# An opening in another order: when k is turned, how filter block 0 is transformed, and where square roots and means stand in GpSimd's queue

## The chip, the cores and the metric

The kernel runs on one core of a Trainium2 chip. The core has five engines with a queue each: TensorE (PE, matrix products; its weight loads are listed apart as PEld), VectorE (DVE), ScalarE (ACT), GpSimd (POOL) and SyncE (SP, which here only issues transfers). They wait for one another by semaphores, and each works through its own queue in order. The metric is the device time of one execution in microseconds; a comparison uses the median of several runs. The working dtype is bf16, sums are float32.

## The reference

Four layers follow one another on x of 2048 tokens by 576 channels: A, B, A, B, each added to its input after a layer norm.

```python
def _A_ref(q, k, v, shift_k, ssm_k, ssm_D):      # k, v, ssm_k, ssm_D are the same in both A layers
    k_shift = sum over 4 taps of k moved by t tokens * shift_k[:, tap]
    kv = k_shift * v
    y = causal convolution of kv with ssm_k along the 2048 tokens, by FFTs of length 4096
    return q * (y + kv * ssm_D)
def _B_ref(x, w_gate, w_up, w_down):             # 576 -> 4608 -> 576
    return (gelu(x @ w_gate) * (x @ w_up)) @ w_down
x = x + _A_ref(_layernorm(x), ...);  x = x + _B_ref(_layernorm(x), ...)    # and both once more
```

## The kernel before, in words

**Units.** The tokens are cut into four chunks of 512. A unit is one B layer of one chunk, eight in all: (layer 0, chunk 0), (0,1), (1,0), (1,1), (0,2), (0,3), (1,2), (1,3). They go in five passes (the first unit alone, three passes of two, the last alone); a pass has three phases, in which its units follow one another; in a phase 12 column groups of `w_gate` and `w_up` are multiplied (L1294, tile `gu`: 18 products each, two at a time in the two halves of the rows), ACT makes the gelu (L1298), DVE multiplies (L1299, tile `hT`), and `w_down` follows (L1311, tile `dn`), four token groups of 24 products, added to the residual `x_c` by DVE (L1345, in the last phase L1340). The first phase of the first unit is cut into two halves of the tokens (`first_half`, `half_gu`, L1228), so that it can begin with two of the four token groups, j = 0 and 2.

**The convolution.** Class `Conv` makes y, which depends on k, v and the filter alone, once per chunk, for both A layers. Chunk m is transformed by products with a twiddle table W (`fwd_full` L207: 8 products of 288 columns give one part, s = 0 or 1, of one of four frequency groups kt, and ACT evicts it, L209; `fwd_eo` L217 makes even and odd sums instead, 4 products for half the channels, from which DVE makes groups kt and kt + 2 by `cross`, L225). Transformed blocks of kv (`kc`) and of the filter (`h0`, `H1`, later `hc`) are multiplied on DVE (`prod`, L234 to L238) and inverted (`inverse`, L276). Blocks needed later are stored in HBM by POOL (L286) and come back as `kr` (L402) and `hr` (L410).

**The order** is written when the program is built. For the opening it is the text of `begin` and `first_half`. From the fourth pair of column groups on (after the change, the third) a planner (`fill`) keeps a rough clock for PE, DVE and ACT and takes from queues what it takes to be ready: `run_loads` (transfers; before the change as many as are ready at once), `run_v` (DVE work of the convolution), `run_p` (its PE work, with tiles from `cps`), `run_aq` and `run_vq` (norms and gates). PSUM is split into a pool `psp` of three tiles that `gu`, `dn` and most of the opening take in turn, and a pool `cps` of one.

**The opening before** (`begin`, L605 on; times of the profiled execution). PE: 32 products of 16 columns (L641), which only keep it busy; the taps' broadcasts (L645); 20 idle products with the identity (L655); the turn of k, 20 transposes (L670); the first half of filter block 0 turned (L690, tile `hps`, copied to `hT` by ACT, L691); the four taps of the short convolution (L565) in three groups; the second half of block 0 turned; then groups 0 and 2 of filter block 0 by even and odd sums (`h0_pair`, L739, with eight crosses on DVE), groups 0 and 2 of kv, and groups 1 and 3 of block 0 and of kv in full (L207); filter block 1 turned (L690); its group 2; the four inverses of chunk 0 (L276, mt = 0, 2, 1, 3).

**The tail of the opening.** For token group j: DVE's `gate` is two operations (L1163: x minus mean, times y; L1165: times rstd plus x, with the row sum). POOL's `mean` makes `nm` from the sum (L934). ACT's `sq` sums squares (L942). POOL's `root` is two operations (L949 `ve`, L950 `rstd`). DVE's `norm` makes `xn` (L1119, L1121), PE turns it (L1132, tile `xps`, after idle transposes L1129), and it is copied to `xnT` (L1140). Before the change `gate` issues its mean itself, and the queues stand thus:

```python
            head.gate(0, Y[0])
            head.gate(2, Y[2])
            head.sq(0)
            ...
            head.gate(1, Y[1])
            ...
            head.root(0)
            head.norm(0)
```

so that POOL has the means of groups 0, 2 and 1 ahead of the root of group 0. Last in `begin`, `head.more(3)` issues the load of the next chunk's x (`load_x(1)`, L889) on POOL, ahead of the roots of groups 1 and 3.

Of the kernel before, what the change touches and what calls it, by code (L numbers as in the profile page):

```python
# [16 lines left out]
ALU = mybir.AluOpType  # L17
# [66 lines left out]
class Conv:  # L84
# [9 lines left out]
    def __init__(self, tc, ctx, pace, A_k, A_v, A_shift_k, A_ssm_k, A_ssm_D, ident, psp, cpsp, ypool):  # L94
# [29 lines left out]
        self.startup = True  # L124
# [231 lines left out]
    def step(self, m, kv=None, loaded=False):  # L356
# [166 lines left out]
    def run_loads(self):  # L523
# [4 lines left out]
        while self.L and self.L[0][0]() <= t.pe - 0.3:  # L528
            self.L.popleft()[1]()
# [19 lines left out]
    def run_p(self):  # L549
# [4 lines left out]
        if max(ready(), self.ps_free) > t.pe:  # L554
            return False
        self.Pq.popleft()
        run()
        t.pe += cost
# [9 lines left out]
    def h1_rest(self):  # L568
# [26 lines left out]
        for s in range(2):  # L595
            for h in range(2):
                self.Pq.append((lambda: NEVER if self.neo >= N_EO else 0.0, 0.49, fwd(s, h)))
        for s in range(2):
            self.Pq.append((lambda: 0.0, 0.98, full(s)))

    def begin(self, head, tables):
# [4 lines left out]
        with ExitStack() as es:  # L606
# [4 lines left out]
            ones = tmp.tile([1, P], BF16, name="ones")  # L611
            warm = tmp.tile([P, 1], F32, name="warm")
# [13 lines left out]
            nc.scalar.dma_start(out=dvec[:], in_=self.sD.unsqueeze(0))  # L626
            nc.vector.memset(ones[:], 1.0)
# [11 lines left out]
            ps = self.ps()  # L639
            for _ in range(32):  # L640
                nc.tensor.matmul(ps[:, 0, 0:16], lhsT=ones[:], rhs=ones[:, 0:16], start=True, stop=True)  # L641
            for j in (3, 2, 1, 0):
# [3 lines left out]
                nc.scalar.copy(out=self.halves(self.skc[:, j, :]), in_=ps[:, :, 0:HW])  # L646
# [6 lines left out]
            ps = self.ps()  # L653
            for _ in range(20):
                nc.tensor.matmul(ps[:, 0, 0:P], lhsT=self.ident[:], rhs=self.ident[:], start=True, stop=True)  # L655
# [75 lines left out]
            def h0_pair(s, h):  # L731

                if s == 0 and h == 0:
                    h0[0] = self.hrp.tile([P, 2, D], BF16, tag="hr", name="h0")
                    h0[2] = self.krp.tile([P, 2, D], BF16, tag="kr", name="h0")
                ps = self.ps()
                for e in range(2):
                    for i in (e, e + 2):
                        nc.tensor.matmul(ps[:, e, 0:HW], lhsT=self.fwd_w(0, s, i), rhs=hT0[:, i, h * HW:(h + 1) * HW],  # L739
                                         start=(i == e), stop=(i == e + 2))  # L740
                eo = self.eop.tile([P, 2, HW], F32, tag="eo", name="eo")
                nc.scalar.copy(out=eo[:], in_=ps[:, :, 0:HW])
                cols = slice(h * HW, (h + 1) * HW)
                self.cross(eo, h0[0][:, s, cols], h0[2][:, s, cols])
                if s == 1 and h == 1:
                    for kt in (0, 2):
                        self.spill(self.Hd[0][kt], h0[kt])

# [9 lines left out]
            for s in range(2):  # L758
                for h in range(2):
                    h0_pair(s, h)  # L760
            kfwd(0)
            head.act_sum(2)
            head.act_sum(3)
            self.load_k(1, nc.gpsimd)
            head.stats(0)
            kfwd(2)
            kacc(0)
            head.act_sq(2)
            for s in range(2):
                h_part(0, 1, s)  # L770
            kfwd(1)
            head.stats(1)
            kacc(2)
            pair0(0, 0)
            head.act_sq(3)
            for s in range(2):
                h_part(0, 3, s)
            kfwd(3)
            self.load_v(1, nc.gpsimd)
            kacc(1)  # L780
            pair0(0, 1)
            self.hT1 = head.scratch([P, RT, D], "hT1")
# [7 lines left out]
            big = lambda: self.psp.tile([P, 2, 512], F32, tag="pr", name="ps")  # L790
            Y = {mt: inv0(mt, big()) for mt in (0, 2)}
            pair0(1, 1)
            Y[1] = inv0(1, big())
            Y[3] = inv0(3, self.cpsp.tile([P, 2, 512], F32, tag="cps", name="cps"))
# [605 lines left out]
```

## Time and profile before

| what | value |
|---|---|
| median of 3 runs | 946.57 us (945.75 to 946.74) |
| the profiled execution's own time | 949.34 us |
| its span, first to last instruction | 947.6 us |
| instructions in the profile | 19593 |
| first product of `w_gate` and `w_up` (L1228) | 46.19 us |
| first product of the second phase (L1294) | 93.67 us |
| DVE busy, ACT busy, POOL busy | 567.1, 292.8, 141.4 us |

The time of one execution is 1.74 us more than its span, for what lies around the first and the last instruction. A page of the profile names an instruction by the line of the kernel, its engine and its tiles (`out<-in`). The view of waits gives engine, line, what it waited for, and then the time in all, how often, and the longest wait. The chain is followed backwards from the last instruction: each piece is what ended last. The view by stretches gives for each stretch its length, the busy time of each engine with the number of instructions, and after them PEclk, the clock that TensorE was granted as a share of full speed.

### The profile page before, as it was taken

The page shows a single profiled execution, that of the slowest core. Times are in us where ns is not written, and L with a number is a line of the kernel's source. Part 1 is how long each engine was busy: PE and PEld are TensorE (multiplying, and loading weights), DVE is VectorE, ACT ScalarE, POOL GpSimd, SP SyncE. Part 2 cuts the span into 40 slices and gives each one's busy share as a digit, 9 for nine tenths or more (in the row PEclk, how much of TensorE's full clock was granted, in tenths as well). Part 3 has the DMA queues.
Part 4 walks back from the last instruction along what each step waited for, and adds up shares of the span by engine and source line. Part 5 has one row for each costly group of instructions (what it writes and reads, how often), then busy time and mean ns, then how long its engine had stood idle before and what let it go on. Part 6 is the DMA issues. An engine that isn't in the chain of part 4 may idle for free.

```text
span 947.6 us, 19593 instructions
## 1 busy us (share of the span) xinstructions
PE 930.1 (98%) x8380; PEld 547.3 (58%) x8380; DVE 567.1 (60%) x1032; ACT 292.8 (31%) x540; POOL 141.4 (15%) x305
## 2 busy tenths in 40 slices
PE   9899999999999998999999999999999999999998
PEld 6677455554654745656556556456456456556455
DVE  4879887888897346888888423763333334533332
ACT  5664315523124333331222521441211213311211
POOL 1433003602103005122010100130000002100000
PEclk9999999999999999999999999999999999999999
DMA  9939987977834515864960720692540540696630
GB/s 258 346 122 240 220 200 145 239 174 193 207 120 88 116 51 149 159 174 106 200 201 13 143 84 26 109 172 47 110 116 1 117 110 14 121 215 148 150 70 26
DMA packets 128491, 130.27 MB, mean 137 GB/s; under 512 B 43538, under 2 KB 120339, under 8 KB 128404
## 3 DMA queue, kind: packets, MB, share of 16 engines
q1 hardware_dynamic: 119232, 93.47, 46.5%
q0 software_dynamic: 9168, 35.54, 11.8%
q8 instruction: 65, 1.06, 0.5%
q14 instruction: 22, 0.18, 0.1%
q10 hardware_dynamic: 4, 0.01, 0.0%
HBM read 107.76 MB, written 11.80 MB: 126 GB/s over the span
## 4 chain that ended last, share of the span: by engine, by line
PE 92%; POOL 2%; DVE 2%; DMA 2%; issue 1%; ACT 1%; DVEq 0%
PE gu L1294 55%; PE dn L1311 27%; PE cps L217 2%; PE gu L1228 2%; DMA wd<-in_B_w_down_dram 2%; PE cps L276 1%; POOL rstd L950 1%; PE ps L207 1%; DVE x_c L1340 1%; PE cps L207 1%; POOL ve L949 0%; ACT junk L942 0%; DVE x_c L1165 0%; ACT hT L691 0%; DVE x_c L977 0%
## 5 line engine op out<-in xcount | busy, mean ns | idle before, releaser
L1294 PE MATMUL gu<-xnT,wgu 64*128 64x512 bf16 x4968 | 542.7, 377 | 4.4 <-DVE x_c L1340 4.4
L1294 PEld LDWEIGHTS <-wgu 64*128 64x128 bf16 x4968 | 244.1, 94 | 296.2 <-issue 12.9
L1298 ACT ACTIVATE ga<-gu 128x512 f32<-128x512 f32 x276 | 164.6, 597 | 522.8 <-PE gu L1294 512.1
L1299 DVE TENSOR_TENSOR hT<-ga,gu 128x512 bf16<-128x512 f32 x276 | 189.4, 686 | 213.4 <-ACT ga L1298 212.4
L1311 PE MATMUL dn<-wd,hT 128*128 128x288 bf16 x2304 | 295.3, 287 | 2.6 <-DMA wd<-in_B_w_down_dram 2.0
L1311 PEld LDWEIGHTS <-hT 128*128 128x128 bf16 x2304 | 224.0, 98 | 69.1 <-issue 12.7
L1345 DVE TENSOR_TENSOR x_c<-x_c,dn 128x576 f32<-128x576 f32 x64 | 48.2, 753 | 79.2 <-PE dn L1311 78.7
L934 POOL TENSOR_SCALAR nm<-s 128x1 f32<-128x1 f32 x62 | 20.3, 328 | 305.4 <-DVE x_c L1340 174.5
L942 ACT ACTIVATE junk<-x_c,nm 128x576 bf16<-128x576 f32 x48 | 37.0, 771 | 47.1 <-POOL nm L934 46.7
L950 POOL TENSOR_TENSOR rstd<-ve,neghalf_t 128x1 f32<-128x1 f32 x62 | 39.5, 637 | 5.2
L220 ACT ACTIVATE eo<-cps 128x576 f32<-128x576 f32 x44 | 28.5, 649 | 34.5 <-PE cps L217 30.1
L410 POOL DMA_DIRECT2D hr<-Hd x32 | 17.3, 539 | 138.6 <-DVE prod L237 138.6
L238 DVE TENSOR_TENSOR sum<-prod 128x576 bf16<-128x576 bf16 x72 | 33.0, 458 | 2.5
L1331 DVE TENSOR_TENSOR ob<-x_c,dn 128x576 bf16<-128x576 f32 x15 | 11.2, 754 | 26.4 <-PE dn L1311 19.6
L1228 PE MATMUL gu<-xnT,wgu 64*128 64x256 bf16 x432 | 25.6, 270 | 0.7 <-DVE xnT L1140 0.7
L1228 PEld LDWEIGHTS <-wgu 64*128 64x128 bf16 x432 | 20.2, 94 | 5.3 <-issue 2.7
L949 POOL TENSOR_SCALAR ve<-ss 128x1 f32<-128x1 f32 x62 | 19.0, 306 | 28.6 <-ACT junk L942 28.4
L291 POOL DMA_DIRECT2D out_dram<-ob x12 | 6.6, 554 | 100.8 <-DVE ob L1331 98.2
L977 DVE SCALAR_TENSOR_TENSOR x_c<-g_t,rstd,x_c 128x576 f32<-128x576 f32 x16 | 13.1, 816 | 14.3 <-POOL rstd L950 14.2
L225 DVE TENSOR_TENSOR kc<-eo 128x288 bf16<-128x288 f32 x48 | 19.3, 454 | 2.2 <-ACT eo L220 2.2
L217 PEld LDWEIGHTS <-W 128*128 128x128 bf16 x176 | 16.8, 99 | 5.8 <-issue 1.3
L470 DVE TENSOR_TENSOR zs<-zs,sum 128x576 f32<-128x576 f32 x24 | 18.1, 755 | 0.4
(129 smaller groups left out, 521.3 us busy)
## 6 DMA issues: line engine op xcount, KB each, us to landing
wgu<-in_B_w_gate_dram SPq DMA_DIRECT2D x45, 576.0 KB, 5.9
wd<-in_B_w_down_dram SPq DMA_DIRECT2D x30, 864.0 KB, 6.7
wgu<-in_B_w_up_dram SPq DMA_DIRECT2D x45, 512.0 KB, 7.7
hr<-Hd POOLq DMA_DIRECT2D x32, 288.0 KB, 4.2
kr<-Kd POOLq DMA_DIRECT2D x24, 288.0 KB, 4.7
Kd<-kc POOLq DMA_DIRECT2D x12, 288.0 KB, 4.7
k<-in_A_k_dram POOLq DMA_DIRECT2D x3, 1008.0 KB, 10.6
wgu<-in_B_w_up_dram SPq DMA_DIRECT2D x45, 64.0 KB, 7.3
```

What stands on the lines that cost most here:

```text
L217: nc.tensor.matmul(ps[:, e, 0:HW], lhsT=self.fwd_w(kt, s, i), rhs=src[:, i, h * HW:(h + 1) * HW], start=(i == e), stop=(i == e + 2))
L220: nc.scalar.activation(out=eo[:], in_=ps[:, :, 0:HW], func=ACT.Copy, scale=scale)
L238: nc.vector.tensor_tensor(out=dst, in0=pr[:, 0, :], in1=pr[:, 1, :], op=ALU.subtract if part == 0 else ALU.add)
L934: nc.gpsimd.tensor_scalar(out=v["nm"][:], in0=v["s"][:], scalar1=-1.0 / D, scalar2=None, op0=ALU.mult)
L942: nc.scalar.activation(out=junk[:], in_=get_x(), func=ACT.Square, bias=v["nm"][:, 0:1], accum_out=v["ss"][:])
L950: nc.gpsimd.tensor_tensor(out=v["rstd"][:], in0=ve[:], in1=neghalf_t[:, 0:1], op=ALU.pow)
L1228: nc.tensor.matmul(pair[:, s, e * 256:(e + 1) * 256], lhsT=w[r0:r0 + HK, k, gi * P:(gi + 1) * P], rhs=xnT[r0:r0 + HK, blk_of[k], tok], sta ...
L1294: nc.tensor.matmul(pair[:, s, :], lhsT=w[r0:r0 + HK, k, gi * P:(gi + 1) * P], rhs=xnT[r0:r0 + HK, b, :], start=(k == 0), stop=(k == NKC - 1))
L1298: nc.scalar.activation(out=ga[:], in_=pair[:, 0, :], func=ACT.Gelu_apprx_tanh)
L1299: nc.vector.tensor_tensor(out=hT[:, fi, :], in0=ga[:], in1=pair[:, 1, :], op=ALU.mult)
L1311: nc.tensor.matmul(acc[:, h, 0:HW], lhsT=hT[:, fi, at * P:(at + 1) * P], rhs=wd[2 * wb + fi // WT][:, fi % WT, h * HW:(h + 1) * HW], start ...
L1345: nc.vector.tensor_tensor(out=xh, in0=xh, in1=acc[:, :, 0:HW], op=ALU.add)
```

## The change

It reorders the opening, and three rules of the planner change with it. Cut to its core:

```diff
 def ps(self):
-        if self.startup and self.nps % 4:
+        if self.other or self.startup and self.nps % 4:
             return self.psp.tile(...)
         return self.cpsp.tile(...)

 # step(): the transforms of kv, half h of the channels
+            if h == 1:
+                self.Pq.extend(self.between)      # groups 1 and 3 of filter block 1, by even and odd sums
+                self.between = []

 # run_loads()
-        while self.L and self.L[0][0]() <= t.pe - 0.3:
-            self.L.popleft()[1]()
+        for _ in range(2):
+            if self.L and self.L[0][0]() <= t.pe - 0.3:
+                self.L.popleft()[1]()

 # run_p(other=False): with other, the tile is one of psp's

 # h1_rest(): groups 1 and 3 go to self.between, group 0 in full stays first

 # begin()
+            nc.vector.memset(full[:], 1.0)        # 128x512
-            for _ in range(32):
-                nc.tensor.matmul(ps[:, 0, 0:16], lhsT=ones[:], rhs=ones[:, 0:16], start=True, stop=True)
+            busy(3, self.ps())                    # 3 products of 512 columns, 128 rows
-                nc.scalar.copy(out=self.halves(self.skc[:, j, :]), in_=ps[:, :, 0:HW])
+                (nc.scalar.copy if n % 2 else nc.vector.tensor_copy)(out=self.halves(self.skc[:, j, :]), ...)
-            for _ in range(20):
-                nc.tensor.matmul(ps[:, 0, 0:P], lhsT=self.ident[:], rhs=self.ident[:], start=True, stop=True)
+            busy(2, self.ps())
+            taps(DBS[0])
             turn_h(0, hT0, 0)
-            taps(DBS[0])
+            turn_h(0, hT0, 1)
             taps(DBS[1])
             taps(DBS[2])
-            turn_h(0, hT0, 1)
-            for s in range(2):
-                for h in range(2):
-                    h0_pair(s, h)
-            kfwd(0) ... kfwd(2) ... h_part(0, 1, s) ... kfwd(1) ... h_part(0, 3, s) ... kfwd(3)
+            tile(0) ... tile(2) ... tile(1) ... tile(3)   # tile(kt): h_part(0, kt, 0), h_part(0, kt, 1), kfwd(kt)
...
             head.gate(0, Y[0])
-            head.gate(2, Y[2])
+            head.mean(0)
+            self.keep_y(0, 2, Y[2])
+            self.keep_y(0, 1, Y[1])
+            head.gate(2)
+            head.mean(2)
             head.sq(0)
+            head.root(0)
+            head.sq(2)
+            head.root(2)
             self.keep_y(0, 0, Y[0])
-            head.sq(2)
-            self.keep_y(0, 2, Y[2])
-            head.gate(1, Y[1])
-            self.keep_y(0, 1, Y[1])
-            head.root(0)
             head.norm(0)
             head.turn(0, 24)
-            head.root(2)
             head.copy(0, nc.scalar.copy)
+            head.gate(1, None, 0)                 # L1163 of group 1 alone
             head.norm(2)
-            head.turn(2, 8)
-            head.copy(2, nc.vector.tensor_copy)
-            head.sq(1)
+            head.turn(2, 8, True)                 # into two tiles of psp
+            head.copy(2, nc.vector.tensor_copy, nc.scalar.copy)
             self.keep_y(0, 3, Y[3])
-            head.more(3)

 # first_half()
-            root0(1)
+            gate0(1, None, 1)                     # L1165 of group 1
+            mean0(1)
+            sq0(1)
             gate0(3)
-            sq0(3)
-            norm0(1)
+            mean0(3)
             for n in range(FP // 2):
                 half_gu(hT, n, 0)
                 if n == 0:
+                    root0(1)
+                    sq0(3)
+                    norm0(1)
+                elif n == 1:
                     root0(3)
                     norm0(3)
-                elif n < 3:
-                    j = 2 * n - 1
-                    turn0(j, 0, cpsp.tile(...))
+                    load_x(1)
+                elif n < 4:
+                    j = 2 * n - 3
+                    turn0(j)                      # a tile of psp

 # dn, in the middle of a token group, while chunk 1's convolution is not done
+                        if fi == FP // 2 and hurry():
+                            conv.run_p(True)
```

The inverses Y[2], Y[1] and Y[0] take their tiles of `psp` in that order, and Y[3] the one of `cps`; the order of the products is as before. SP's queue has the same transfers in the same order in both programs.

More of the change, by code (lines that the diff above doesn't have):

```diff
@@ L547, in run_v, with run_p @@
         return True
-    def run_p(self):
+    def run_p(self, other=False):
         t = self.t
@@ L553, in run_p @@
         ready, cost, run = self.Pq[0]
-        if max(ready(), self.ps_free) > t.pe:
+        if max(ready(), 0.0 if other else self.ps_free) > t.pe:
             return False
         self.Pq.popleft()
+        free, self.other = self.ps_free, other
         run()
+        if other:
+            self.ps_free, self.other = free, False
         t.pe += cost
@@ L611, in begin @@
             ones = tmp.tile([1, P], BF16, name="ones")
+            full = tmp.tile([P, 512], BF16, name="full")
             warm = tmp.tile([P, 1], F32, name="warm")
@@ L637, in begin, with busy @@
             head.more(1)
-            ps = self.ps()
-            for _ in range(32):
-                nc.tensor.matmul(ps[:, 0, 0:16], lhsT=ones[:], rhs=ones[:, 0:16], start=True, stop=True)
-            for j in (3, 2, 1, 0):
+            def busy(n, ps):
+                for _ in range(n):
+                    nc.tensor.matmul(ps[:, 0, :], lhsT=full[:, 0:P], rhs=full[:], start=True, stop=True)
+            busy(3, self.ps())
+            for n, j in enumerate((3, 2, 1, 0)):
                 ps = self.ps()
@@ L729, in pair0 @@
                     self.yb[(part, kt, sg)] = b
[L731 to L747, printed above, removed]
             def inv0(mt, ps):
@@ L1183, in more @@
                     load_wgu(n)
-            elif k == 3:
-                load_x(1)
         head = SimpleNamespace(
             zero=neghalf_t[:], more=more, stats=lambda j: [run() for _, _, run in g0[2 * j:2 * j + 2]],
-            act_sum=act_sum0, act_sq=act_sq0, gate=gate0, sq=sq0, root=root0, norm=norm0, turn=turn0, copy=copy0,
+            act_sum=act_sum0, act_sq=act_sq0, gate=gate0, mean=mean0, sq=sq0, root=root0, norm=norm0, turn=turn0, copy=copy0,
             scratch=lambda shape, name: xtp.tile(shape, BF16, tag="xnT", name=name),
```

89 lines of the change are left out of this document (47 added, 42 removed).

## The prediction

> **What bounds the kernel now.** First the page's busy times and the waits of TensorE, its engine column PE:
>
> ```profile
> PE 930.1 (98%) x8380; PEld 547.3 (58%) x8380; DVE 567.1 (60%) x1032; ACT 292.8 (31%) x540; POOL 141.4 (15%) x305
> ```
>
> ```profile
> PE gu L1294 <- DVE x_c L1340: 4.4, 3, 3.5
> PE xps L1132 <- DVE xn L1119: 2.5, 2, 1.8
> PE dn L1311 <- DMA wd<-in_B_w_down_dram: 2.0, 1, 2.0
> ...
> PE xps L1129 <- ACT y L282: 1.1, 1, 1.1
> PE ps L739 <- ACT hT L691: 1.0, 1, 1.0
> ...
> PE gu L1228 <- DVE xnT L1140: 0.7, 1, 0.7
> ```
>
> PE is busy 98%, so only its idle time and its own work count. Of some 14 us of waits, 6.1 lie in the opening (L739, L1129, L1132, L1228, and 0.8 at L207, left out here). Two lie later: 2.0 at 199 us (the load of `w_down`) and 3.5 at 369 us. Then the stretches behind these two (length, PE, PEld, DVE, ACT, POOL, then PEclk):
>
> ```profile
> 201.00:204.60 3.60, 3.58 (x16) 2.25 (x16) 0.76 (x2) 0.65 (x1) 0.00 (x0) 0.53 0.89 171
> 371.80:375.30 3.50, 2.77 (x14) 1.19 (x15) 3.46 (x8) 2.22 (x5) 2.25 (x6) 0.51 0.86 296
> ```
>
> Behind each, the clock was about half for 3.5 us: 1.7 us more each. Last the chain through the tail of the opening:
>
> ```profile
> 41.23 0.84 DVE x_c L1165 x2
> 42.06 0.07 issue
> 42.14 0.21 POOL nm L934
> 42.34 0.16 POOL ve L949
> 42.51 0.07 issue
> 42.58 0.58 POOL rstd L950
> 43.15 0.03 issue
> 43.18 0.59 DVE xn L1119
> 43.77 0.05 issue
> 43.81 0.69 PE xps L1132 x9
> ```
>
> The first root (L949, L950) comes right behind a mean (L934) that waited for DVE's third gate. Its own squares were done at 39.97 (ACT, L942). Here 2 us lie open.
>
> **The change, part by part** (durations of the profiled execution).
>
> *Start.* Before: tiny products from 1.09, taps' broadcasts 2.27 to 4.70, 20 idle products 2.25, k's turn 6.95 to 9.22. k had landed at 0.73 + 4.2 = 4.93. After: the first product waits for a memset of 128x512, which the trace lacks: between 0.13 (the memset of one row) and 0.41 (a copy of 128x512 bf16); I take 0.25, so PE starts at 1.2. A cold 512-column product is 0.44 (288 columns took 0.25): three end at 2.5, broadcasts (2.43) 4.95, two more 5.85, k's turn (2.27) 8.1: 1.1 earlier. Copies of two taps go to DVE, which stood idle to 5.35; `dg` and `kT` are still done before 8.1 (k's first copy ended 0.9 + 1.0 after the turn began). Nothing.
>
> *The taps ahead of the filter's turns.* The first taps took 1.85 at full clock. The clock opened near 10.0: the identity products take 313 ns each before it, the same 128 columns 219 ns in L565 after. So 1.9 us of the taps run at half speed and do 0.95 of the work; they end at 10.9. Two turns of block 0 at 1.00 each: 12.9. Two groups of taps (2.29): 15.2; meanwhile ACT's two copies (1.12 each, from 11.95) end at 14.2, so the wait of 1.0 at L739 goes.
>
> *Block 0 in full.* 8 products (0.98) for each of 16 groups: 15.7 us, to 30.9. Before, the groups went from 16.8 to 30.58, with 16 products fewer (1.96). The front thus loses 0.3. ACT has 16 evictions at 0.55 to 0.65 and 3.1 us of sums and squares in it, some 12.7 of 15.7, and with four PSUM tiles no group waits for it. The eight crosses (3.04) leave DVE; they gain nothing, since DVE was done at 36.06 and the first inverse at 36.55, behind ACT's copies of block 1 (31.49 to 33.64), which stay. First inverse: 36.85.
>
> *Tail.* Roots of 0 and 2 stand behind the means of 0 and 2 only. DVE's first two gates end at 40.40 in the trace, the second mean starts 40.48; root 0 ends 1.01 after the start of the mean ahead of it (42.14 to 43.15): 41.49, plus 0.3: 41.8. Behind it `norm` (turn 0.63 later, 42.45 to 43.15; ACT's copies 1.1, to 44.25). On DVE `norm` (0.8), the half gate (0.74), second `norm` at 43.35 (its root ends 1.0 after the first, 42.8, in time); turn 43.98; DVE's copy of five blocks from 44.4 (0.49), ACT's of four from 44.7 (0.60). First gu at 45.2, before 46.19: 1.0 earlier. In all this stands a gap of 0.47 that the chain calls "issue" ahead of the first L1165; the other gates show 0.04 there and nothing is waited for, so I take it as gone: first gu at 44.8, 1.4 earlier, with 1.0 as the other end. ACT's extra evictions of y[2], y[1] end at 39.5 and hold the first squares by 0.1 at most.
>
> *First half.* Root 1 stood behind the load of x (L889), which waited 4.9 us on POOL for the fourth gate; the load now comes behind both roots. `xn` of group 1 is ready near 49.2, PE comes to its turn after three pairs (6.2) at 51.0. The wait of 0.76 goes, with 1.8 us to spare. In `psp` every tile of the first half has its reader done two or more us ahead (third tile back: DVE's product of the first pair at 48.6). The load of x goes out near 49.4 instead of 49.02, its readers (L927) start after 57.
>
> *The rest.* PE's products behind the first gu are the same in number and form. The first transform of kv moves ahead from 73.5 to about 62.7 (seven pairs at 2.07, two turns and two groups behind the first gu); by the rows of L182, L187, L192 and L1232 DVE has its half of kv about 1.4 us before it. Two groups more fit into `dn` with `psp` tiles; their crosses are done before the tile comes round. At nothing: DVE idles up to 2 us at each phase's start (96.5, 131.7), which is the cover. **Loads by twos** looks like the cure for the wait at 369 us, where POOL issues six loads ahead of two roots:
>
> ```profile
> 368.73 0.54 POOL L410 DMA_DIRECT2D hr<-Hd  x1
> 369.28 0.20 POOL L949 TENSOR_SCALAR ve<-ss 128x1 f32<-128x1 f32 x1
> 369.57 0.57 POOL L950 TENSOR_TENSOR rstd<-ve,neghalf_t 128x1 f32<-128x1 f32 x1
> 370.12 0.18 POOL L949 TENSOR_SCALAR ve<-ss 128x1 f32<-128x1 f32 x1
> 370.39 0.55 POOL L950 TENSOR_TENSOR rstd<-ve,neghalf_t 128x1 f32<-128x1 f32 x1
> ```
>
> DVE's gate (L977) starts at 370.97, behind the second. In the new order POOL has four loads, one root, two loads, the other root: the same sum. The 3.5 us stay. SP's order is unchanged, all that it waits for there hangs on PE, so the 2.0 at 199 us stay too.
>
> **Sum:** 1.4 + 0.76 = 2.2. The profiled execution would go from 949.34 (span 947.6 and 1.74 around it) to 947.2. It lies 2.77 above the median, and I carry that difference over: **944.4 us**. Its ends: 0.4 for the gap, 0.15 for the memset, and for the clock, which may open up to 1.9 earlier or somewhat later, 0.6; about 0.9 to either side. About 0.2% (1.9 us) is what a measurement can tell from no change, so the forecast ends close by that bound.
>
> **Rivals.**
>
> 1. *The clock opens a window later*, at 13.4 (the half-clock stretches above are 3.4 long). Then the rest of the taps and two turns run cold: 0.9 and 0.2 more, 945.5. For it: 20 idle products became two. Against: in the trace a window with hardly more than transposes (6.95 to 10.4) opened it. [...]
>
> 2. *The clock falls in the tail.* PE idles in three pieces between 41.2 and 44.8 (about 0.9, 0.5, 0.4) with 2 us of transposes between. If one window counts as idle, 3.4 us at half follow: 1.7 back, 946.1. Before, 1.77 and 0.68 idle in the same place had no such effect; 2.05 at 199 us had. [...]
>
> 3. *The weight load does not move.* If the 2.0 at 199 us is set by bandwidth and not by its issue at 186.75 (14.2 us to landing), PE arrives 2.2 earlier and waits 2.2 longer: 946.6. Against: its issue and its neighbours' all follow PE.
>
> 4. *One of the two half-clock stretches vanishes*, because the idle time falls across two windows: 1.7 more, 942.7.
>
> 5. *Slower.* The clock needs the removed idle products: windows that mix transposes, short waits and long products do not open it until the groups of block 0 run. Each window of such work at half speed costs 1.7 us, the first 1.1; opening at 20 us costs 4.5: 948.9. It decides between the second window (2.8) and the third, where it passes the gain and 0.2% (4.1). Against: from 8.1 on PE has no wait at all.
>
> **Chances:** forecast 0.68 (its own range 943.5 to 945.3; 0.46 of it beyond the bound of 944.7), rival 1 0.10, 2 0.07, 3 0.04, 4 0.07, 5 0.04. Faster by over 0.2%: 0.46 + 0.07 = 0.53; within: 0.22 + 0.10 + 0.07 + 0.04 = 0.43; slower 0.04. The range leaves out rivals 3 and 5 and the outer ends: 942.7 to 946.2.
>
> **What would show it.** First gu near 44.8 and L1294's first product near 91.5 (46.19 and 93.67 before); no wait at L739; one wait at `xps` of about 0.9 instead of two of 1.8 and 0.8; the first root on POOL right behind the second mean; waits of 2.0 and 3.5 still there, with half clock behind them. A first gu at 46 or later, a new wait in the first half, or another length of the two late waits would make the prediction wrong.

## The result, and the profile after

The changed kernel took **944.27 us** in the median of 16 runs (941.27 to 944.98), the kernel before 946.0 us (16 runs on the same chip, 943.43 to 947.53). The ratio is 0.9977, with a 95% interval of 0.9968 to 0.9985: faster by 0.23%. The forecast was 944.4. The profiled execution of the changed kernel took 944.51 us (span 942.7).

The page's busy times, and the view of waits of PE, of the changed kernel (line numbers move: L1342 was L1340; L1159 was L1165; L924, L939 and L940 were L934, L949 and L950; L1109 was L1119; L1125 was L1132; L1132 was L1140):

```profile
PE 929.8 (99%) x8349; PEld 547.9 (58%) x8349; DVE 565.4 (60%) x1026; ACT 293.0 (31%) x539; POOL 140.2 (15%) x305
```

```profile
PE gu L1294 <- DVE x_c L1342: 4.6, 3, 3.6
PE ps L649 <- DVE full L634: 1.5, 1, 1.5
PE xps L1125 <- DVE xn L1109: 1.2, 2, 0.9
...
PE gu L1294 <- DVE ob L1333: 0.6, 1, 0.6
...
PE gu L1228 <- DVE xnT L1132: 0.5, 1, 0.5
```

PE does nearly the same work. The wait at L739 is gone, as the prediction said; those at `xps` fell from 2.5 to 1.2, in two pieces of 0.9 and 0.3 where it said one of about 0.9. The wait for x_c of 3.5 is still there, as 3.6. Three things were not foretold: the wait for y (L282) is gone, the wait for the load of `wd` is gone, and there is a new one, of `gu` for `ob`.

The chain through the tail of the opening:

```profile
39.36 0.84 DVE x_c L1159 x2
40.20 0.07 issue
40.27 0.21 POOL nm L924
40.48 0.16 POOL ve L939
40.64 0.07 issue
40.71 0.58 POOL rstd L940
41.29 0.03 issue
41.31 0.59 DVE xn L1109
```

The root (L939, L940) stands right behind the second mean. Before, DVE's third gate lay between, and `xn` began at 43.18.

PE's stretches behind the wait at 362 us (columns as before: length, PE, PEld, DVE, ACT, POOL, PEclk, DMA share, GB/s), and POOL in front of them:

```profile
360.70:364.15 3.45, 1.30 (x13) 0.48 (x9) 0.11 (x1) 0.05 (x1) 3.10 (x7) 1.00 0.95 261
364.15:367.50 3.35, 1.90 (x10) 0.82 (x11) 3.32 (x9) 2.22 (x5) 1.52 (x4) 0.50 0.76 279
367.50:371.00 3.50, 3.50 (x18) 1.39 (x16) 2.72 (x6) 0.60 (x1) 0.74 (x2) 0.50 0.43 84
```

```profile
361.46 0.57 POOL L940 TENSOR_TENSOR rstd<-ve,neghalf_t 128x1 f32<-128x1 f32 x1
361.99 0.61 POOL L402 DMA_DIRECT2D kr<-Kd  x1
362.60 0.54 POOL L410 DMA_DIRECT2D hr<-Hd  x1
363.16 0.20 POOL L939 TENSOR_SCALAR ve<-ss 128x1 f32<-128x1 f32 x1
363.45 0.56 POOL L940 TENSOR_TENSOR rstd<-ve,neghalf_t 128x1 f32<-128x1 f32 x1
```

Four loads, a root, two loads, a root: the sum foretold. PE idles 2.15 of the first stretch, and the clock is half for the next two (6.83 us in the trace's record of the clock). A "half-clock stretch" below is one such piece of 3.41 us; in the profile of before there was one here.

**Where the time went.** From the starts of PE's phases in the two traces (a phase is all of `gu` or all of `dn` of a unit), spans 947.6 and 942.7:

| stretch | before | after | gain |
|---|---|---|---|
| start to the first `gu` (L1228) | 46.19 | 44.51 | 1.68 |
| first `gu` to the second phase's first L1294 | 47.48 | 46.00 | 1.48 |
| the `dn` near 199 us, to the next `gu` | 19.67 | 15.79 | 3.88 |
| the `gu` near 362 us (369 before), to its `dn` | 28.41 | 29.83 | -1.42 |
| the `gu` near 832 us (838 before), to its `dn` | 23.42 | 24.22 | -0.80 |

They make 4.82 of 4.85; every other phase is alike within 0.02. The experiments below show that only the first two and the last belong to the change.

### The profile page after: what moved, and what is told of

Read it like the earlier page. It is cut to its first block, busy times and chain, and to the rows that moved or that the text cites. A ratio compares the mean times of both kernels' runs of the same rounds, so it can differ in the third digit from the quotient of the medians.

```text
span 942.7 us, 19524 instructions
## 1 busy us (share of the span) xinstructions
PE 929.8 (99%) x8349; PEld 547.9 (58%) x8349; DVE 565.4 (60%) x1026; ACT 293.0 (31%) x539; POOL 140.2 (15%) x305
## 3 DMA queue, kind: packets, MB, share of 16 engines
q1 hardware_dynamic: 119232, 93.47, 45.6%
q0 software_dynamic: 9168, 35.54, 11.2%
## 4 chain that ended last, share of the span: by engine, by line
PE 90%; issue 3%; DVE 2%; POOL 2%; DMA 1%; ACT 1%; DVEq 0%; POOLq 0%; ACTq 0%
PE gu L1294 54%; PE dn L1311 26%; PE gu L1228 3%; PE cps L217 2%; PE ps L207 1%; PE cps L276 1%; POOL rstd L940 1%; DMA out_dram<-ob 1%; PE cps L207 1%; DVE x_c L1342 1%; POOL ve L939 0%; ACT junk L932 0%; DVE x_c L967 0%; POOL nm L924 0%; PE hps L697 0%
## 5 line engine op out<-in xcount | busy, mean ns | idle before, releaser
L1294 PE MATMUL gu<-xnT,wgu 64*128 64x512 bf16 x4968 | 544.2, 377 | 5.2 <-DVE x_c L1342 4.6
L1294 PEld LDWEIGHTS <-wgu 64*128 64x128 bf16 x4968 | 245.5, 94 | 297.0 <-issue 15.7
L1311 PEld LDWEIGHTS <-hT 128*128 128x128 bf16 x2304 | 223.6, 98 | 66.1 <-issue 10.5
L924 POOL TENSOR_SCALAR nm<-s 128x1 f32<-128x1 f32 x62 | 20.0, 322 | 308.5 <-DVE x_c L1342 174.5
L940 POOL TENSOR_TENSOR rstd<-ve,neghalf_t 128x1 f32<-128x1 f32 x62 | 38.9, 628 | 5.2
L1228 PE MATMUL gu<-xnT,wgu 64*128 64x256 bf16 x432 | 25.1, 269 | 0.5 <-DVE xnT L1132 0.5
L939 POOL TENSOR_SCALAR ve<-ss 128x1 f32<-128x1 f32 x62 | 18.5, 299 | 34.1 <-ACT junk L932 34.0
L1228 PEld LDWEIGHTS <-wgu 64*128 64x128 bf16 x432 | 21.0, 94 | 4.1 <-issue 2.3
```

Source lines behind the costliest of these rows:

```text
L924: nc.gpsimd.tensor_scalar(out=v["nm"][:], in0=v["s"][:], scalar1=-1.0 / D, scalar2=None, op0=ALU.mult)
L940: nc.gpsimd.tensor_tensor(out=v["rstd"][:], in0=ve[:], in1=neghalf_t[:, 0:1], op=ALU.pow)
L1228: nc.tensor.matmul(pair[:, s, e * 256:(e + 1) * 256], lhsT=w[r0:r0 + HK, k, gi * P:(gi + 1) * P], rhs=xnT[r0:r0 + HK, blk_of[k], tok], sta ...
L1294: nc.tensor.matmul(pair[:, s, :], lhsT=w[r0:r0 + HK, k, gi * P:(gi + 1) * P], rhs=xnT[r0:r0 + HK, b, :], start=(k == 0), stop=(k == NKC - 1))
L1311: nc.tensor.matmul(acc[:, h, 0:HW], lhsT=hT[:, fi, at * P:(at + 1) * P], rhs=wd[2 * wb + fi // WT][:, fi % WT, h * HW:(h + 1) * HW], start ...
```

## The experiments

Each run lists its mean granted clock. In the profiles 1.000, 0.998 and 0.996 stand for none, one and two half-clock stretches behind the opening; so times can be compared at the same number of them. "The opening of the clock" is the moment at which the trace's record of full clock begins.

**1. Does the second profile say the same?** The changed kernel again, and the kernel before again, nothing edited.

> The changed kernel once more, unaltered. My theory: the 2.05 us wait of dn (L1311) for the load of wd at 199 us, which the profile of before has and that of after has not, is a chance of one profiled execution (there the two turns that SP issues ahead of the load took 5.9 us, here 3.6), and so is the number of half-clock stretches behind the wait at 362 us (one or two of 3.4 us, 1.7 us each). So here: no wait of dn for wd or one under 1 us, the wait at 362 us of 3.4 to 3.7 again, first product of the second phase (L1294) at 90.5 +- 0.3, and a time of 942.5 to 945. Rival: the change itself moved the load; then nothing in this run differs from the profile of after, and only a second profile of before tells the two apart.

> The kernel before, unaltered, profiled a second time. My theory: the 2.05 us wait of dn for the load of wd at 199 us and the half-clock stretch behind it (3.88 us together from the start of that dn to the next gu: 19.67 against 15.79 in every other profile) were a chance of the first profiled execution; here dn to gu takes 15.79, and the time is 943.5 to 946.6 instead of 949.34. The stretch from the first gu to the second phase's first L1294 stays at 47.5 (33.17 + 14.31), 1.5 longer than the 46.0 of the changed kernel. Rival: the wait belongs to the order of before, then it is here again, at 1.5 to 2.5 us, and the change has removed it.

The changed kernel: 942.53 us in the median, no wait for `wd`, the wait for x_c 3.6 again, one stretch of half clock behind it. Its first L1294 came at 91.52, 1.0 later than expected, since the first `gu` came at 45.52. The clock opened at 11.23 here and at 9.17 in the first profile: the first `gu` moves by half of that difference.

The kernel before: 945.63 us in the median. The wait for `wd` is not there, `dn` to `gu` takes 15.79, first `gu` to L1294 47.49. Its waits of PE:

```profile
PE gu L1294 <- DVE x_c L1340: 4.4, 3, 3.5
PE xps L1132 <- DVE xn L1119: 2.5, 2, 1.8
PE ps L641 <- DVE kT L628: 1.1, 1, 1.1
```

So the 3.88 was a chance of one execution, and the rival that the change moved that load falls. There are two stretches of half clock at 367 us in this profile of before too: their number is not the change's either. By that number the runs stand thus (mean, and the number of runs; "before" are the runs of the kernel before that were made beside the experiments, "changed" the first 16 and the 10 of this experiment):

| half-clock stretches | before | changed | difference |
|---|---|---|---|
| none (1.000) | 943.65 (21) | 941.56 (8) | 2.1 |
| one (0.998) | 945.7 (39) | 943.9 (10) | 1.8 |
| two (0.996) | 946.5 (16) | 944.6 (8) | 1.9 |

Over all of these runs, whatever their number of stretches, the means are 945.3 and 943.4: again 1.9. The eight runs of the kernel before in this experiment are not in the table; with them no mean of it moves by 0.1.

**2. The tail: means ahead of roots again.**

```diff
             head.mean(2)
+            head.gate(1)
+            head.mean(1)
             head.sq(0)
             head.root(0)
...
-            head.gate(1, None, 0)
...
-            gate0(1, None, 1)
-            mean0(1)
```

> The changed kernel with one thing undone: the whole gate of group 1 (L1163, L1165) and its mean stand ahead of the root of group 0 again on DVE and POOL; PE's, ACT's and SP's order is untouched. My theory (the tail's order carries the first gu's 1.68 us): the third gate takes DVE 0.9 + 0.9 and its mean 0.2 on POOL ahead of the root, so the first root ends 1.2 to 1.6 us later, the first gu (L1228) moves from 44.5 to 45.7-46.1, and the time is 1.2 to 1.6 us more (0.1 to 0.2%), 945.5 +- 0.5. Rival (the front, k's early turn and block 0 in full, carries the gain): first gu at 44.5 +- 0.3 and the time within 0.4 us of the changed kernel. A second rival: the first gu is later, but the second phase's first L1294 comes at 90.5 all the same, because the first half waits for something else.

945.92 us against 942.53 for the changed kernel run beside it. First `gu` at 47.03 with the clock opening at 10.32; the changed kernel would have it at 45.1 there (table below), so 1.9 later, where 1.2 to 1.6 were expected. The rest is in the waits and the clock:

```profile
PE xps L1126 <- DVE xn L1110: 2.5, 1, 2.5
```

```profile
41.00:44.46 3.46, 0.93 (x18) 0.76 (x16) 2.07 (x5) 1.40 (x3) 2.42 (x6) 1.00 1.07 380
44.46:47.87 3.41, 3.13 (x31) 2.52 (x30) 1.25 (x3) 2.24 (x5) 0.00 (x0) 0.50 0.83 276
```

PE is idle 2.5 us in one piece, and the clock is half from 44.46 to 47.87: the prediction's rival 2, which the changed kernel, with 0.9 and 0.3 in two pieces, escapes. The rival that the front carries the gain falls. The edit moves DVE's third gate as well as POOL's mean. In its trace DVE is done with that gate at 42.34 and then stands idle for 1.13 until the root, which stands behind the mean; in the changed kernel `xn` would begin at 41.9 at this opening. So of the 1.6 by which `xn` (43.47) is late, some 1.1 is the root's place behind the mean, and the rest is DVE's own gate. No run moved the one without the other.

**3. The front as before**, with the tail and the planner as changed.

```diff
-            busy(3, self.ps())
+            for _ in range(32):
+                nc.tensor.matmul(ps[:, 0, 0:16], lhsT=ones[:], rhs=ones[:, 0:16], start=True, stop=True)
...
-            taps(DBS[0])
             turn_h(0, hT0, 0)
+            taps(DBS[0])
...
-            turn_h(0, hT0, 1)
...
-            tile(0)
...
+            turn_h(0, hT0, 1)
+            for s in range(2):
+                for h in range(2):
+                    h0_pair(s, h)
+            kfwd(0)
```

> The changed kernel with the front of before: tiny and identity products as fillers, taps copied by ACT alone, the order of turns and taps, groups 0 and 2 of filter block 0 by even and odd sums with crosses, and the order of the groups; the tail and the planner's rules as changed. My theory: the front is worth nothing, the first inverse starts between 36.4 and 37.0 (36.75 in the changed kernel, 36.55 before), the first gu between 44.1 and 44.9, and the time is within 0.5 us of the changed kernel. Rival (the front carries the gain): the first gu at 45.5 or later and the time 1 us or more above the changed kernel. Second rival (block 0 in full costs what the 16 products more take, 1.96 us, without a return): the first gu at 43.5 or earlier and 1 us less.

942.93 us against 942.53; the first `gu` at 45.18 with the clock opening at 10.75, where the changed front gives 45.3. For the first `gu` the front is worth nothing, as forecast (45.18 is later than the 44.1 to 44.9 that was expected, since the clock opened 1.6 later than in the first profile). The first inverse ends at 36.99; the times of it in the text above are ends as well. This nothing is a sum of two things, as the chain shows, first here and then in the kernel before:

```profile
37.90 0.47 issue
38.37 0.84 DVE x_c L1177 x2
```

```profile
37.45 0.47 issue
37.91 0.83 DVE x_c L1165 x2
```

The gap of 0.47 ahead of the first gate's second half is there in all four profiles with the front of before, this one with the changed tail among them; in the nine with the changed front (run 4 with the old fillers too) it is 0.04. So the gap goes with the order of the front's groups and not with the tail, though the prediction had it in the tail's sum. Against that, the first inverse starts here at 35.84, about 0.5 earlier than with the changed front at the same opening. What the gap is, no view shows.

This kernel has no wait for `ob` near 832 us (23.42 there). At one half-clock stretch its runs are at 942.7 (8 runs), the changed kernel's at 943.9; at two, 944.7 (3 runs) and 944.6. So the times leave open how much of that wait they show.

**4. The fillers alone as before**: no `full`, 32 tiny and 20 identity products, all taps copied by ACT.

```diff
-            nc.vector.memset(full[:], 1.0)
...
-            busy(3, self.ps())
+            for _ in range(32):
+                nc.tensor.matmul(ps[:, 0, 0:16], lhsT=ones[:], rhs=ones[:, 0:16], start=True, stop=True)
...
-            busy(2, self.ps())
+            for _ in range(20):
+                nc.tensor.matmul(ps[:, 0, 0:P], lhsT=self.ident[:], rhs=self.ident[:], start=True, stop=True)
```

> The changed kernel with the old fillers: no memset of `full`, 32 tiny and 20 identity products, all four taps copied by ACT; order otherwise as changed. My theory: k's turn goes back from about 6.1 to about 6.9 but the clock's opening does not hang on the fillers (it opened between 9.2 and 11.2 in four profiles with them); first gu within 44.3 to 45.6, 0 to 0.8 later than the changed kernel at the same opening of the clock. The rival on the clock (long products warm it sooner): it opens one stretch of 3.4 us later than with `full`, at 12.5 or later, and the first gu is 0.9 or more later. A second question: all four profiles with this front show a wait of gu for ob (L1333) of 0.6 to 1.0 us near 832 us, and the dn phase there takes 24.1 to 24.4 us; the two with the front of before take 23.42. If that hangs on the tile `full` (another place of all later tiles in memory), it goes here; if it hangs on the order of the front's groups, it stays.

The clock opened at 10.75, inside what the changed kernel shows (8.69 to 11.23 with its front in eight profiles): the rival on the clock falls. First `gu` at 45.75 (expected up to 45.6), 0.45 later than with `full` at the same opening; k's turn began at 7.02 instead of 6.1. The wait for `ob` is gone here too. The time, 946.18 us, is spoilt by something else:

```profile
PE dn L1310 <- DMA wd<-in_B_w_down_dram: 6.0, 1, 6.0
```

Of 12 runs five took 948.8 to 955.7. The load that PE waits for was issued 9.1 us ahead of its `dn` and took 17.7 to land. In the first profile of before it was 9.6 ahead and took 14.2; in the eleven profiles without the wait it took 10.5 to 12.0 (issued 11.9 ahead in the changed kernel and in the second profile of before). The turn of `xn` (L1022) that SP issues right behind it was slow as well: 12.03 here, 7.26 and 4.84 in the two profiles of before. So PE waited where this load went out late and landed slowly, while SP's transfers were slow around it; why this kernel meets that so often, and before once, was not found out.

First `gu` against the opening of the clock, in profiles with the changed front and tail:

| clock's record begins | 8.69 | 9.17 | 10.25 | 10.45 | 10.55 | 11.23 |
|---|---|---|---|---|---|---|
| first `gu` | 44.27 | 44.51 | 45.03 | 45.13 | 45.18 | 45.52 |

Over these six profiles 2.54 us of later opening cost 1.25 us, a half. The kernel before had 46.19 at 10.04 and 45.81 at 8.86; at the same openings the table gives 44.93 and 44.36. The opening's gain at equal clock is thus 1.3 to 1.45.

**5. The planner's places undone.**

```diff
         for s in range(2):
+            for h in range(2):
+                self.Pq.append((lambda: NEVER if self.neo >= N_EO else 0.0, 0.49, fwd(s, h)))
+        for s in range(2):
             self.Pq.append((lambda: 0.0, 0.98, full(s)))
-        self.between = [...]
+        self.between = []
...
-                        if fi == FP // 2 and hurry():
-                            conv.run_p(True)
```

> The changed kernel with the groups of filter block 1 in their old places: groups 1 and 3 by even and odd sums ahead of the second half of kv, and no groups with tiles of psp within dn. My theory (each group put between pairs of gu costs 0.6 there and breaks the stream of gu, but 0.49 in dn): the stretch from the first gu to the second phase's first L1294 goes from 46.0 to 46.7, and the time rises by 0.7 us against runs of the changed kernel with the same number of half-clock stretches. Rival (the places cost nothing, and the 0.7 came with the early psp tiles or the first half): the stretch stays at 46.0 +- 0.15 and the time within 0.3. Second rival (the first transform of kv comes too late or too early and PE waits for DVE's half of it): 48 or more.

First `gu` to L1294 took 46.43 (46.00 changed, 47.48 before). So the places are worth 0.43 of that stretch; 0.76 is the wait of the first half, which stays away here; 0.29 remains. Of it the trace of this run shows 0.22: a turn of `xn` and the group right behind it take 1.10 together, twice; before, with a pair of column groups between, they take 0.61 and 0.60. In time the kernel is at 942.4, 943.7 and 945.8 with none, one and two half-clock stretches (4, 2 and 6 runs): 0.9 more, 0.2 less, 1.2 more than the changed one. With so few runs at each number the stretch is the firmer measure.

**6. All ready loads at once.**

```diff
-        for _ in range(2):
-            if self.L and self.L[0][0]() <= t.pe - 0.3:
-                self.L.popleft()[1]()
+        while self.L and self.L[0][0]() <= t.pe - 0.3:
+            self.L.popleft()[1]()
```

> The changed kernel with all ready loads issued at once again instead of two at a time. My theory: nothing moves; the wait of gu for x_c (L1342) near 362 us is 3.5 +- 0.15 against 3.6, since POOL has the same six loads and two roots ahead of the same gate, and the time is within 0.5 us at the same number of half-clock stretches. Rival: taking loads by twos spread them and saved some of that wait; then it is 4.2 or more here. Second rival: it is shorter, 3.0 or less, since the two roots then stand together.

The wait is 3.5 instead of 3.6, and the time 943.82 us (941.5, 944.0 and 944.5 with none, one and two half-clock stretches, within 0.1 of the changed kernel). Loads by twos did nothing here.

**7. Loads held back while a gate waits for its root.** As long as the next gate in the queue belongs to group 2 of that unit, POOL gets no load.

```diff
+    def gate_near():
+        need = vq[0][0] if vq else 0.0
+        g = None if isinstance(need, float) else need[3] if need[0] == "y2" else need[1]
+        return g is not None and any(g is hvars.get(1, {}).get(j) for j in (2,))
...
-        conv.run_loads()
+        conv.run_loads(hold=gate_near())
...
-    def run_loads(self):
+    def run_loads(self, hold=False):
...
-        for _ in range(2):
+        for _ in range(0 if hold else 2):
```

> The changed kernel with POOL's transfers held back while the gate of the next unit's first-used group waits for its root: at 358 to 364 us POOL then has the two roots ahead of the six loads, no instruction more or fewer. My theory (POOL's loads, 0.54 each, keep the root from DVE's gate L977, and PE waits 3.6 at gu L1294 for x_c): the wait of 3.6 goes or falls under 0.6 us, and with it one or two half-clock stretches of 1.7 us each; the time falls by 3.5 to 6.5 us to 938 to 941. Rival (what limits there is the chain of squares, root and norm, the loads only fill POOL's idle time): the wait stays at 3 us or more and the time within 1 us. Second rival (the loads held back come late): the wait at 362 us goes, and prod or the inverse waits for hr or kr some us later, so that less than 2 us is left of the gain.

940.12 us (939.92 to 940.52), no half-clock stretch in any run. POOL, and PE's waits around it (340 to 385 us):

```profile
360.70 0.18 POOL L939 TENSOR_SCALAR ve<-ss 128x1 f32<-128x1 f32 x1
360.97 0.55 POOL L940 TENSOR_TENSOR rstd<-ve,neghalf_t 128x1 f32<-128x1 f32 x1
362.47 0.22 POOL L924 TENSOR_SCALAR nm<-s 128x1 f32<-128x1 f32 x1 [0.95 <-DVE x_c L967]
362.68 0.63 POOL L402 DMA_DIRECT2D kr<-Kd  x1
```

```profile
PE gu L1299 <- DVE x_c L1347: 0.6, 1, 0.6
PE gu L1299 <- DVE hT L1304: 0.6, 1, 0.6
```

Both roots are done at 361.5, the loads follow, and nobody waits for them. The phase takes 25.04 instead of 28.68 (one half-clock stretch) or 29.83 (two). The loads were the cause; both rivals fall. Against the changed kernel's runs without a half-clock stretch (941.56) the gain is only 1.4, where the waits differ by 2.4. By the table above such runs may be those whose clock opened early, which is worth up to 1.2. An estimate from the traces agrees: the stall lies at 362.0 to 365.6 with an opening at 9.17 and moves by half of the opening, while the place where half clock began in five profiles, 354.98 behind the opening (last section), moves by the whole; with an opening near 8.5 that place falls in the middle of the stall, with 1.8 idle on either side. No profile caught such a run, so this stays open.

**8. The wait for `ob` near 832 us.** All six profiles with the five long fillers had it, the four with the old ones had not. Either the place of `full` in memory, or the number of PE's instructions.

```diff
-                    nc.tensor.matmul(ps[:, 0, :], lhsT=full[:, 0:P], rhs=full[:], start=True, stop=True)
-            busy(3, self.ps())
+                    nc.tensor.matmul(ps[:, 0, 0:64], lhsT=full[:, 0:P], rhs=full[:, 0:64], start=True, stop=True)
+            busy(24, self.ps())
...
-            busy(2, self.ps())
+            busy(16, self.ps())
```

> The changed kernel with the five fillers of 512 columns cut into 40 of 64 (24 and 16), as many columns in all, and the same tile `full` and memset: 35 products and 35 weight loads more in PE's stream, nothing else. Open: the wait of gu for ob (L1333) of 0.6 to 1.0 us near 832 us, which all profiles with the new fillers have (dn there 24.1 to 24.4 us) and the four with the old ones have not (23.42). In the former the trace shows a fetch of 16 KB of instructions 10.9 to 11.2 us behind the start of that dn, where the store of ob (L291), which ob waits for, is under way (10.5 to 13.7); in the latter it comes at 5.0 to 8.1, ahead of it. My theory: the number of PE's instructions ahead decides, since it sets when the fetch falls; then here the fetch comes at 8 to 10 and the dn takes 23.42 to 23.9; the time is 0.3 to 0.9 less than the changed kernel's at the same number of half-clock stretches. Rival: the place of the tile `full` in memory decides; then fetch or no fetch, the dn takes 24.1 or more and the time is the same.

The wait is gone: 23.42, with the tile where it was. What DVE waited for ahead of `ob`, in the changed kernel (826 to 836 us) and in this one (825 to 835):

```profile
DVE ob L1333 <- DMA out_dram<-ob: 7.0, 1, 7.0
```

```profile
DVE ob L1333 <- DMA out_dram<-ob: 5.5, 1, 5.5
```

And the DMA queues at the moment of the fetch of instructions (packets, MB, share), 831.4 to 832.8 in the changed kernel, 824.5 to 826 in this one:

```profile
q0 software_dynamic: 76, 0.21, 44.5%
...
q8 instruction: 1, 0.02, 5.8%
```

```profile
q1 hardware_dynamic: 312, 0.31, 107.5%
q8 instruction: 1, 0.02, 5.6%
```

q0 carries what POOL issues (35.54 MB on the page, the sum of POOL's transfers), the stores among it. In the changed kernel the fetch falls among the stores' packets; here it comes 4.9 us behind the start of `dn` (8 to 10 were expected, and 11.1 it is in the changed kernel), when no packet of q0 moves yet. The store lands 1.5 earlier, and PE needs not wait. Over all profiles the store that `ob` waits for lands in 9.4 to 9.7 us in the six with the wait and in 7.9 to 8.5 in the seven without. That the number of PE's instructions decides, and not the place of `full`, is shown. That it does so through this fetch is argued only: the two move together, but in the changed kernel the store's packets already begin 10.6 behind the start of `dn`, ahead of the fetch, and here at 9.7. The time is 943.69 us: 940.9, 943.3 and 944.0 with none, one and two stretches (2, 2 and 6 runs), 0.6 to 0.7 less than the changed kernel at each.

**9. Both together.** The loads held back (run 7) with the cut fillers (run 8), and with the front of before (run 3); no other edit. (In the two texts below the "fourth", "third" and "sixth" are runs 7, 3 and 4 here, and "the run before" is run 8.)

> POOL's transfers held back as in the fourth run (median 940.12, no half-clock stretch, dn near 832 us of 24.12) together with the cut fillers of the run before. If the cut moves the fetch of instructions out of the store's way: 939.3 to 939.8. If it does not: 940.1 +- 0.3. If holding the loads helped only by a chance of the clock's windows, some runs show half-clock stretches and lie at 941.5 or more.

> POOL's transfers held back as in the fourth run, with the front of before as in the third (which had no wait near 832 us and a first gu 0.1 earlier at the same opening of the clock). By the third and fourth runs: 940.12 less 0.8 for ob less 0.1 to 0.3 for the front: 938.9 to 939.3, against a kernel before of about 945.5. If the two do not add (the front of before needs its stall at 362 us for nothing, but other waits appear): 940 or more. If the wait of dn for wd near 199 us comes up in it, as in 5 of 12 runs of the sixth kernel, which has the same fillers: single runs of 943 or more.

938.84 us (938.53 to 939.64) and 938.74 us (938.68 to 939.56), ratios to the kernel before 0.9936 (0.9921 to 0.9951) and 0.9935 (0.9922 to 0.9948). Both beat both kernels and lie below what was expected, by 0.5 and 0.2; no run showed half clock, or a wait for `wd` in the profile. The two reach the same time with opposite fronts, which says again that the front as a whole is worth nothing.

## Why the prediction was right, step by step

- *Start.* The memset of 128x512 took 0.48, not 0.25 (even the upper end, 0.41, was short). PE began at 1.51 instead of 1.2, k's turn at 6.09 instead of 5.85. k's turn is 0.6 earlier than before, and little hung on it.
- *The clock "opened near 10.0".* It opened at 8.69 to 11.23 over the profiles. At 9.17 the groups of block 0 began at 14.93; forecast was 15.2, for an opening near 10.0. Rivals 1 and 5 did not come; with 40 fillers (run 8) it opened at 10.55, with 52 (run 4) at 10.75, both inside the range of the profiles with five. In run 3 the 3.41 us ahead of the opening (7.34 to 10.75) hold transposes alone, and the clock opened behind them, as the prediction held against rival 1.
- *"The front thus loses 0.3."* At the same opening the first inverse starts 0.4 to 0.65 later than before, so this term was too small. Yet with the tail as changed, the front of before has its first `gu` only 0.1 earlier, since the changed front also loses the gap of 0.47.
- *Tail: 1.4.* From the first inverse to the first `gu` 8.91 instead of 10.80; less what the front loses, 1.3 to 1.45. The gap of 0.47 that the prediction "took as gone" is gone, but by run 3 for a reason of the front. With the front of before the changed tail brings the first `gu` from about 46.5 to 45.18 at an opening of 10.75 (the 46.5 is an estimate, carried on from 46.19 at 10.04): some 1.3, with the gap still there. The prediction's own terms give the same: 1.0, and the 0.3 of the front that it had taken off. So the tail's mechanism and size were right; the front's loss was too small by 0.2, and the gap stood in the wrong part of the sum.
- *First half: 0.76.* Gone, with no new wait in its place.
- *"At nothing" for the planner's places* was mis-sized: 0.43 of gain in the stretch to the first L1294, and 0.29 more there, 0.22 of it from turns that stand next to a group. The reason seen in the trace is that a pair of column groups with nothing between takes 2.00 to 2.04, and a group put between costs 0.60 instead of the 0.49 that it takes in `dn`. The prediction counted products and left out these 0.11 a group.
- *Loads by twos, the 3.5 at 369 us.* As forecast: same sum on POOL, the wait stays. Held back altogether, the loads free 1.4 to 4.4 us (940.2 against 941.56 to 944.6).
- *"The 2.0 at 199 us stay too"* failed: the wait was a chance of one profile. By the prediction's list another length of it was a sign of error; the second profile of before, which lacks the wait too, takes that sign away. Rival 3 is not met either, but its doubt was sound: this load landed in 10.5 to 17.7 us over the profiles, so its landing does not simply follow its issue.
- *The missing term.* Nothing in the prediction asked what fewer PE instructions do to the transfers 800 us later. The wait for `ob` gave 0.8 back in the first profile; without it (run 8) the runs are 0.6 to 0.7 faster.
- *The sum, 2.2.* Measured at equal numbers of half-clock stretches: 1.8 to 2.1. It is 1.3 to 1.45 for the opening, 1.48 for the first unit, less 0.8. That 944.4 came so close to 944.27 is luck in two ways. Two terms that it did not have, +0.72 and -0.80, cancel. And it stood on 946.57, the median of three runs; over 16 it is 946.0, so that by medians the gain is 1.73, not 2.2. Carrying over the 2.77 by which the profile lay above the median was sound: it was the wait for `wd` and its half clock (3.88), less what other runs lose at 369 us.
- What rivals 2 and 4 describe occurred in other runs: half clock in the tail in the kernel with means ahead of roots (0.50 from 44.46 to 47.87), and no half-clock stretch in some runs of the changed kernel (941.3 to 942.1) and of the kernel before in the table (943.5 to 943.9). That the idle time fell across two windows in those, as rival 4 has it, no profile shows.

## What to carry to other kernels

A short operation that DVE waits for should not stand in GpSimd's queue behind transfers (the wait of 3.6 us that run 7 removed), or behind the means of groups that are needed later (some 1.1 us in run 2); move it first, count what is queued ahead, and hold transfers back for it. Before a stall of one profile goes into a sum, take a second profile of the same kernel (the 3.88 us that were a chance of one execution); compare runs at the same number of clock stretches. When instructions are removed, look for new waits far from the edit as well (the 0.80 near 832 us).

## What the runs showed of the hardware

- Half clock came although the 3.4 us ahead of it were not idle throughout: PE was busy 1.30 of 3.45 in the first profile of the changed kernel (360.70 to 364.15) and 0.93 of 3.46 in run 2 (41.00 to 44.46). By the trace's record it lasted 3.41 us (201.18 to 204.59 and 371.85 to 375.26 in the first profile of before) or 6.83 (364.15 to 370.98 in the first of the changed kernel). Near 365 us it started 354.98 or 354.99 us behind the opening of the clock in the profiles of the changed kernel (openings at 9.17 and 11.23) and of runs 3, 6 and 8 (10.75, 10.45, 10.55), although PE's own work lay up to 1 us apart in them (the first `gu` 34.29 to 35.34 behind the opening); in the second profile of before and in run 5 (openings at 8.86 and 8.69) it started 358.40 behind it, and in the first profile of before (10.04) 361.81. These three distances are 3.42 and 3.41 apart, about the length of one half-clock stretch.
- The opening of the clock varied by 2.5 us between executions (8.69 to 11.23), and the first `gu` moved by half of that (44.27 to 45.52 with the changed front and tail). That is up to 1.25 us by itself, where this change is worth 1.8 to 2.1.
- With 70 PE instructions more at the start (run 8) a 16 KB fetch 800 us later came 4.9 us behind the start of its `dn` instead of 11.1, and the store of 144 KB that `ob` waits for landed in 7.9 to 8.5 us in the profiles with the early fetch and in 9.4 to 9.7 in those with the late one.
- A turn of `xn` by DMA took between 1.31 and 12.03 us to issue on SP in the same place of nearly the same kernel, right behind a load of 864 KB that itself landed in 10.5 to 17.7 us (1.47 and 7.26 in the first profiles of the changed kernel and of before, 12.03 in run 4).
